# Local attention feeding a phase mixer on one core: q and k transposed by column halves, and the first attention and its loads reordered

## The chip, the core and the metric

The kernel runs on one core of one Trainium2 chip. The metric is the device time of one execution in microseconds (us); lower is better. A core has five engines that run beside each other, each through its own list of instructions in order: TensorE for matmuls (PE in the profile; PEld is its loading of weights), VectorE (DVE), ScalarE (ACT), GpSimd (POOL) and SyncE (SP). They meet through semaphores. DMA queues move data between device memory, the on-chip memory SBUF and back; matmul results land in PSUM, from where DVE or ACT must copy them. A tile here is a block of SBUF or PSUM with 128 partitions.

## What is computed

There are 4 batches of 8 heads, 768 tokens and 64 values per head. A token sees the first 8 tokens and the 96 latest ones (itself among them), with a bias that falls with the distance by a slope of the head. The attention's output, 512 wide, goes through a phase layer, a mix over tokens and a channel layer:

```python
scores = scale * q @ k.T + bias            # kept where global or local
a = softmax(scores); x = heads_to_columns(a @ v)
theta = x @ w_theta
zr, zi = x * cos(theta), x * sin(theta)
y = w_tok_r @ zr + w_tok_i @ zi            # over the 768 tokens
u = x + y
out = u + relu(u @ w_ch)
```

## The kernel before

Tokens are cut into 6 tiles of 128 and heads into 4 pairs; p is the pair. For a pair, q and k are brought into the form "two heads' 64 values on 128 partitions, tokens along the row" (qT and kT). Scores are made for 128 keys at a time against their own 128 queries and the next 128, with kG holding the keys of a tile with the 8 global keys copied over its first columns (`kglob`). One score block c covers two key tiles of both heads; ACT takes its exponential (`score_exp`, L302). `values` multiplies by v, which carries a column of ones, so that column 64 is the softmax's sum; DVE takes the reciprocal (L360) and multiplies (L362) into x. `xtrans` transposes x, `theta` multiplies by w_theta and takes cosine and sine on ACT (L395) and the products zri on DVE (L398), `mix` multiplies by the token weights (L409), and `utrans` and `chan` do the channel layer.

Batch 0's attention has an order written out by hand for all engines (the statements from `load_w()` to `manual.close()`). There the bias goes into PSUM as a matmul with a diagonal matrix (`diagonals`, `score_bias`, L275), ahead of the score matmuls (L295), which use the two halves of the array's rows, one head each. For pair 0, q and k come as fp32 through SP's and ACT's queues and are cast by DVE and ACT (`cast0`, L198); for pairs 1 to 3, they come as bf16 through POOL's queue, and `cast0` is a copy on DVE that puts the two heads beside each other per token tile. Then `turn0` (L204) transposes 128 x 128 blocks into PSUM, 6 for q and 6 for k, and `out0` (L211) copies them out, kT on ACT and qT on DVE. The bias tables for the later batches (`bias_table`, L142, eight activations) stand at the end, after the sines of batch 0.

Batch 1 to 3 are woven into the mixing of the batch before by `weave`, which deals side steps out by weights in proportion to the main steps; from `manual.close()` on a scheduler sets each engine's order within that, and `behind` keeps a preparation after the latest mix on its engine. Batches 1 and 2 prepare q and k with `prep`: `prep_copy` (L229, two DVE copies per pair, a pair ahead), 12 transposes (L244), the copies out (L249 on DVE, L251 on ACT) and `kglob` (L218, L220). Both batches' preparations fall into the mixing of batch 0. Batch 3 uses DMA transposes (`prep_dma`). Transposed blocks, mix sums and batch 0's values share four small PSUM buffers; score blocks use two large ones.

All large loads go through POOL's queue in program order: q, k, v of batch 0 by pieces, w_theta, the token weights (`load_w`, L159: three loads of two token tiles for each of the two matrices), w_ch (L162), then q and k of batch 1, v of batch 1, q and k of batch 2. A load waits for the one eight places before it. `trans_w` (L168, L169) transposes the token weights; tile 0 before theta, the others between mixes.

Of the kernel before, what the change touches and what calls it, by code (L numbers as in the profile page):

```python
# [9 lines left out]
FP = mybir.dt.float32  # L10
BF = mybir.dt.bfloat16
AF = mybir.ActivationFunctionType
# [4 lines left out]
def kernel(  # L17
# [13 lines left out]
    nc = tc.nc  # L31
    B, H, S, D = q.shape
    T = 128
# [103 lines left out]

    etab = const.tile([T, H, 5, T], BF)

    def bias_table(p):  # L140
        for h in (2 * p, 2 * p + 1):
            nc.scalar.activation(etab[:, h], dist[:, 0:5], AF.Exp, scale=-slopes[h])  # L142

    halfpi = const.tile([T, 1], FP)
    junk = const.tile([T, 1], FP)
# [8 lines left out]
    def load_w():  # L154
        nc.gpsimd.dma_start(out=w_theta_bf, in_=moe_w_theta.rearrange("(c p) n -> p c n", p=T))
        for tt in range(0, NT, 2):
            for wi, src in enumerate((moe_w_tok_r, moe_w_tok_i)):
                w2 = moe.tile([T, 2, S], BF, name="w_nat", bufs=6)
                nc.gpsimd.dma_start(  # L159
                    out=w2, in_=src[tt * T:(tt + 2) * T, :].rearrange("(a p) s -> p a s", p=T))  # L160
                w_nat[wi, tt], w_nat[wi, tt + 1] = w2[:, 0], w2[:, 1]
        nc.gpsimd.dma_start(out=w_ch_bf, in_=moe_w_ch.rearrange("(c p) n -> p c n", p=T))  # L162

    def trans_w(tt, copy=nc.vector.tensor_copy):
# [22 lines left out]
    def behind(eng):  # L187

        return tc.issue_after(anchor[eng]) if eng in anchor else nullcontext()

    tiles0 = {}

    def cast0(p, i_, eng, h=None):
        if (p, "n") not in tiles0:
            tiles0[p, "n"] = att.tile([T, NT, 2, 2, D], BF, name="qkn", bufs=2)
        src = qk32[:, i_] if p == 0 else loads[0][0][:, i_, 2 * p:2 * p + 2]
        hs = slice(0, 2) if h is None else slice(h, h + 1)
        eng(out=tiles0[p, "n"][:, :, i_, hs].rearrange("p t h d -> p h t d"), in_=src[:, hs])  # L198

    def turn0(p, i_):  # L200
        qkn = tiles0[p, "n"]
        ps = tiles0[p, i_] = ps_small([T, NT, T], BF)
        for t_ in range(NT):
            nc.tensor.transpose(ps[:, t_, :], qkn[:, t_, i_].rearrange("p h d -> p (h d)"), ident)  # L204

    def out0(p, i_, copy, half=None):
        to = qkT.setdefault((0, p), [None, None, None])
        if to[i_] is None:
            to[i_] = att.tile([T, S], BF, name=("qT", "kT")[i_], tag=("qT", "kT")[i_], bufs=6)
        ns = slice(0, T) if half is None else slice(half * T // 2, (half + 1) * T // 2)  # L210
        copy(out=to[i_].rearrange("p (n t) -> p n t", t=NT)[:, ns],  # L211
             in_=tiles0[p, i_].rearrange("p t n -> p n t")[:, ns])

    def kglob(b, p):
        kT = qkT[(b, p)][1]
        kG = qkT[(b, p)][2] = att.tile([T, NT - 2, T], BF, name="kG", bufs=6)
        with behind("dve") if b == B - 1 else nullcontext():
            nc.vector.tensor_copy(  # L218
                out=kG, in_=kT[:, T:(NT - 1) * T].rearrange("p (t n) -> p t n", t=NT - 2))
            nc.vector.tensor_copy(out=kG[:, :, 0:NG], in_=kT[:, None, 0:NG].to_broadcast([T, NT - 2, NG]))  # L220

    qkns = {}

    def prep_copy(b, p):
        qk = loads[b][0]
        qkn = qkns[b, p] = att.tile([T, NT, 2, 2, D], BF, name="qkn", bufs=2)
        with behind("dve"):
            for i_ in range(2):
                nc.vector.tensor_copy(  # L229
                    out=qkn[:, :, i_].rearrange("p t h d -> p h t d"), in_=qk[:, i_, 2 * p:2 * p + 2])  # L230

    def prep(b, p):
        if p == 0:
            prep_copy(b, 0)
        if p + 1 < NP:
            prep_copy(b, p + 1)
        qkn = qkns[b, p]
        qT = att.tile([T, S], BF, name="qT", bufs=6)
        kT = att.tile([T, S], BF, name="kT", bufs=6)
        for i_, dst in ((0, qT), (1, kT)):  # L240
            ps = ps_small([T, NT, T], BF)
            with behind("pe"):
                for t_ in range(NT):
                    nc.tensor.transpose(ps[:, t_, :], qkn[:, t_, i_].rearrange("p h d -> p (h d)"), ident)  # L244

            dst = dst.rearrange("p (n t) -> p n t", t=NT)
            src = ps.rearrange("p t n -> p n t")
            if i_ == 0:
                nc.vector.tensor_copy(out=dst, in_=src)  # L249
            else:  # L250
                nc.scalar.copy(out=dst, in_=src)  # L251

        qkT[(b, p)] = [qT, kT, None]
        kglob(b, p)
# [78 lines left out]
            nc.vector.tensor_copy(out=vG[:, hs], in_=vn[:, hs, 1:NT - 1, :])  # L333
        nc.vector.tensor_copy(out=vG[0:NG, hs], in_=vn[0:NG, hs, 0:1, :].to_broadcast([NG, n, NT - 2, D + 1]))

    def values(b, p, hh):
        vn = loads[b][1]
        e_t, vG = ebuf[(b, p)], vGs[b]
        h = 2 * p + hh
        if b == 0:  # L340
            po = ps_small([T, 1, 512], FP)
        else:
            if hh == 0:
                pos[(b, p)] = ps_big()
            po = pos[(b, p)][:, hh:hh + 1, :]
        for it in range(NT):
            mms = [(e_t[:, hh, it, 0, :], vn[:, h, it, :])]
            if it:
                mms.append((e_t[:, hh, it - 1, 1, :], vG[:, h, it - 2, :] if it > 1 else vn[:, h, 0, :]))
            o = po[:, 0, it * (D + 1):(it + 1) * (D + 1)]  # L350
            for i_, (l_, r_) in enumerate(mms):
                nc.tensor.matmul(o, lhsT=l_, rhs=r_, start=(i_ == 0), stop=(i_ == len(mms) - 1))  # L352
        if b and hh == 0:
            return
        if b:
            po = pos[(b, p)]
        h0, n = (hh, 1) if b == 0 else (0, 2)
        po4 = po[:, :, 0:NT * (D + 1)].rearrange("p a (t d) -> p a t d", d=D + 1)
        rec = att.tile([T, n, NT, 1], FP, name="rec", tag=f"rec{n}")
        nc.vector.reciprocal(rec, po4[:, :, :, D:D + 1])  # L360
        xv = x_sb[b][:, p, :, h0 * D:(h0 + n) * D].rearrange("p t (a d) -> p a t d", a=n)
        nc.vector.tensor_mul(xv, po4[:, :, :, 0:D], rec.to_broadcast([T, n, NT, D]))  # L362

    def xtrans(b, p, copy=nc.vector.tensor_copy):
        if b:
            anchor["sp"] = nc.sync.dma_start_transpose(
                out=xT_sb[b][:, p, :].rearrange("p (t s) -> p t s", t=NT),
                in_=x_sb[b][:, p].rearrange("p t d -> p (t d)")).ins
            return
        ps = ps_small([T, S], BF)  # L370
        for st in range(NT):
            nc.tensor.transpose(ps[:, st * T:(st + 1) * T], x_sb[b][:, p, st, :], ident)
        copy(out=xT_sb[b][:, p, :], in_=ps)


    zri, u_sb, uTs, pss, css = {}, {}, {}, {}, {}
# [68 lines left out]
    def load_all_qk(b):  # L445
        alloc_qk(b)
        load_qk(b, 0, 8)
# [54 lines left out]
            i_ += 1  # L502

    load_w()
    load_all_qk(1)
    load_all_v(1)
    load_all_qk(2)
    alloc_x(0)
# [1 line left out]
    warm(6)  # L510
    distances()
    diagonals(0)
    cast0(0, 1, dve, 0)
    cast0(0, 1, act, 1)
    turn0(0, 1)
    cast0(0, 0, dve, 0)
    cast0(0, 0, act, 1)
    turn0(0, 0)
    out0(0, 1, act, 0)
    out0(0, 1, dve, 1)  # L520
    out0(0, 0, act, 1)
    out0(0, 0, dve, 0)
    kglob(0, 0)
    score_bias(0, 0)
    score_bias(0, 1)
    score_mms(0, 0, 0)
    score_mms(0, 0, 1)
    score_exp(0, 0, 0)
    cast0(1, 1, dve)
    cast0(1, 0, dve)  # L530
    diagonals(1)
    turn0(1, 1)
    turn0(1, 0)
    for p in range(NP):
        nxt = p + 1 < NP
        score_exp(0, p, 1)
        if nxt:
            out0(p + 1, 1, act)
            out0(p + 1, 0, dve)
            kglob(0, p + 1)  # L540
        if p:
            values(0, p - 1, 0)
            values(0, p - 1, 1)
        score_bias(p, 2)
        score_mms(0, p, 2)
        score_exp(0, p, 2)
        if p + 2 < NP:
            cast0(p + 2, 1, dve)
            cast0(p + 2, 0, dve)
            diagonals(p + 2)  # L550
        if p == 0:
            vglob(0, 0, 4)
        if p == 1:
            vglob(0, 4, 4)
        if nxt:
            score_bias(p + 1, 0)
            score_mms(0, p + 1, 0)
            score_exp(0, p + 1, 0)
            score_bias(p + 1, 1)
            score_mms(0, p + 1, 1)  # L560
            if p + 2 < NP:
                turn0(p + 2, 1)
                turn0(p + 2, 0)
        if p:
            xtrans(0, p - 1, act if p == NP - 1 else dve)
    values(0, NP - 1, 0)
    values(0, NP - 1, 1)
    trans_w(0, nc.scalar.copy)
    xtrans(0, NP - 1)
    for c in range(NT // 2):  # L570
        theta(0, c, 0)
        theta(0, c, 1)
    for p in range(NP):
        bias_table(p)
    manual.close()
    for eng in (mybir.EngineType.PE, mybir.EngineType.DVE, mybir.EngineType.Activation):
        last = [i for i in nc.cur_bb.bb.instructions if i.engine == eng][-1]
# [82 lines left out]
```

The softmax here doesn't subtract the row's maximum and nothing guards it: scores larger than these inputs give would overflow.

## Time and profile before

| | us |
|---|---|
| median of 13 runs (lowest, highest) | 174.99 (174.42, 176.38) |
| profiled execution, its own time | 174.42 |
| its span | 172.4 |
| PE busy | 159.5 (93%) |
| DVE busy | 128.1 (74%) |
| ACT busy | 99.2 (58%) |
| first exponential starts (L302) | 9.37 |
| first theta matmul (L389) | 27.98 |
| first mix matmul (L409) | 33.16 |
| k of batch 1 landed (issued at 22.28) | 41.7 |
| first transposes of batch 1 (L244) | 41.67 |

Times of events are counted from the span's start. In a row of the timeline the numbers are the start and the time from the first start to the last end of a run of like instructions, then engine, line, operation, what is written and what is read, shapes and count; the bracket at the end is idle time before it and what ended it. A row of the groups ends in busy time, the mean of one in ns, and idle time with what ended it. Rows of tenths cut the span into 40 slices, each digit the busy share of one. A matmul's busy time is longer than its slot, since matmuls overlap in the array: slots are read from the distances between starts. The chain of waits follows the work that ended last back to the start.

### The profile page before, as it was taken

Reading aid. Unit: us, or ns where it says so; the run is one execution under the profiler, and the core shown is the slowest. Engines: PE = TensorE matmul, PEld = TensorE weight load, DVE = VectorE, ACT = ScalarE, POOL = GpSimd, SP = SyncE. Lnnn points to the kernel's source line nnn. Section 1 sums busy time; section 2 is a strip of 40 time slices with the busy share of each in tenths; the row PEclk is TensorE's granted clock in tenths of the full one; section 3 lists DMA queues with packets and bytes.
Section 4 is the critical chain, followed back from the end, with each engine's and each line's share of the span. In section 5 each row is a group of like instructions: output and inputs, shape, how many; then the busy total and the mean of one; then the engine's idle time right before and its main releaser. Section 6 shows DMA issues by size and latency. Waiting matters only on the chain.

```text
span 172.4 us, 3627 instructions
## 1 busy us (share of the span) xinstructions
PE 159.5 (93%) x1457; PEld 84.7 (49%) x1482; DVE 128.1 (74%) x288; ACT 99.2 (58%) x124; POOL 37.3 (22%) x45
## 2 busy tenths in 40 slices
PE   6789978999999999999999998999999989999991
PEld 1355655455756566544455463444554634444440
DVE  7578965677999999999587588597786837724443
ACT  2479676999497595489834740989348308500010
POOL 8983346005271110099100000000000000000000
PEclk9999999999999999999999999999999999999999
DMA  5999999999999999899999697787138571313335
GB/s 152 189 194 178 210 208 208 205 204 171 161 204 174 166 156 155 108 110 154 213 134 136 157 161 167 137 152 224 30 76 112 136 171 40 143 40 101 102 93 183
DMA packets 75088, 25.92 MB, mean 150 GB/s; under 512 B 63168, under 2 KB 72128, under 8 KB 75072
## 3 DMA queue, kind: packets, MB, share of 16 engines
q0 software_dynamic: 45680, 12.45, 78.2%
q1 hardware_dynamic: 28976, 12.72, 34.7%
q10 hardware_dynamic: 416, 0.52, 0.9%
q8 instruction: 11, 0.18, 0.4%
q14 instruction: 5, 0.04, 0.1%
HBM read 25.69 MB, written 6.29 MB: 185 GB/s over the span
## 4 chain that ended last, share of the span: by engine, by line
PE 49%; DMA 22%; DVE 19%; POOL 5%; issue 2%; ACT 1%; SPq 0%; DVEq 0%; POOLq 0%
PE ps L409 27%; DMA qk<-in_k_dram 11%; PE ps L434 9%; DMA w_nat<-in_moe_w_tok_r_dram 7%; PE pb L295 4%; PE pb L352 3%; PE pb L389 3%; DVE qT L249 3%; POOL qk L73 3%; DVE e L312 2%; DVE qkn L229 2%; PE ps L389 2%; DVE o_sb L440 2%; POOL vn L88 2%; DMA kT<-qk 2%
## 5 line engine op out<-in xcount | busy, mean ns | idle before, releaser
L409 PE MATMUL ps<-zri,w_tokT 128*128 128x512 bf16 x271 | 67.4, 379 | 1.5 <-issue 0.5
L302 ACT ACTIVATE e<-pb 128x1024 bf16<-128x1024 f32 (+1 forms) x48 | 43.6, 958 | 22.5 <-PE pb L295 22.3
L409 PEld LDWEIGHTS <-w_tokT 128*128 128x128 bf16 x288 | 26.1, 98 | 28.9 <-issue 1.0
L414 DVE TENSOR_TENSOR u<-x_sb,ps 128x512 bf16<-128x512 bf16 x24 | 16.4, 681 | 14.6 <-PE ps L409 12.7
L434 PE MATMUL ps<-w_ch_bf,uT 128*128 128x512 bf16 x94 | 23.9, 379 | 0.3 <-DVE u L414 0.2
L398 DVE TENSOR_TENSOR zri<-x_sb,cs 128x512 bf16<-128x512 bf16 x48 | 17.9, 416 | 7.8 <-ACT cs L395 7.6
L440 DVE SCALAR_TENSOR_TENSOR o_sb<-ps,u 128x512 f32<-128x512 f32 (+1 forms) x25 | 16.4, 661 | 3.1 <-PE ps L434 3.1
L395 ACT ACTIVATE cs<-pb,halfpi 128x1024 bf16<-128x1024 f32 x8 | 8.9, 1115 | 15.7 <-PE pb L389 15.7
L312 DVE TENSOR_TENSOR e<-e,etab 128x1024 bf16<-128x1024 bf16 (+1 forms) x24 | 14.7, 615 | 3.4 <-ACT e L302 3.4
L295 PE MATMUL pb<-qT,kT 64*128 64x128 bf16 x224 | 15.9, 223 | 0.8 <-ACT kT L211 0.3
L389 PE MATMUL pb<-w_theta_bf,xT 128*128 128x512 bf16 x62 | 15.0, 379 | 1.1 <-DMA xT<-x_sb 1.0
L295 PEld LDWEIGHTS <-kT 64*128 64x128 bf16 x224 | 9.0, 95 | 14.2 <-issue 13.0
L389 PEld LDWEIGHTS <-xT 128*128 128x128 bf16 x96 | 9.1, 98 | 11.9 <-DMA xT<-x_sb 2.2
L428 ACT COPY uT<-ps 128x512 bf16<-128x512 bf16 x7 | 4.1, 587 | 18.6 <-PE ps L427 18.6
L352 PEld LDWEIGHTS <-e 128*128 128x128 bf16 x352 | 12.7, 97 | 3.0 <-issue 1.0
L434 PEld LDWEIGHTS <-uT 128*128 128x128 bf16 x96 | 8.9, 98 | 10.0 <-ACT uT L428 0.3
L295 PE MATMUL pb<-qT,kG 64*128 64x128 bf16 x128 | 11.9, 220 | 0.3 <-DVE kG L220 0.3
L88 POOL DMA_DIRECT2D vn<-in_v_dram x5 | 9.6, 1928 | 11.8 <-DVE vn L68 10.2
L362 DVE TENSOR_TENSOR x_sb<-pb,rec 128x768 bf16<-128x768 f32 x12 | 11.4, 948 | 0.3
L315 DVE TENSOR_TENSOR e<-e,etab 128x1024 bf16<-128x1024 bf16 x12 | 8.2, 684 | 2.8 <-ACT e L302 2.8
L352 PE MATMUL pb<-vn,e 128*128 128x65 bf16 x168 | 9.6, 193 | 0.2
L251 ACT COPY kT<-ps 128x768 bf16<-128x768 bf16 x8 | 6.4, 798 | 5.1 <-PE ps L244 5.1
(74 smaller groups left out, 205.5 us busy)
## 6 DMA issues: line engine op xcount, KB each, us to landing
out_dram<-o_sb SPq DMA_DIRECT2D x23, 256.0 KB, 2.4
vn<-in_v_dram POOLq DMA_DIRECT2D x3, 768.0 KB, 22.8
qk<-in_q_dram POOLq DMA_DIRECT2D x2, 768.0 KB, 20.7
qk<-in_k_dram POOLq DMA_DIRECT2D x2, 768.0 KB, 23.4
w_nat<-in_moe_w_tok_r_dram POOLq DMA_DIRECT2D x3, 384.0 KB, 14.2
w_nat<-in_moe_w_tok_i_dram POOLq DMA_DIRECT2D x3, 384.0 KB, 15.4
vn<-in_v_dram POOLq DMA_DIRECT2D x2, 384.0 KB, 8.8
qk<-in_q_dram POOLq DMA_DIRECT2D x8, 96.0 KB, 9.3
```

What stands on the lines that cost most here:

```text
L88: nc.gpsimd.dma_start(out=vn[:, h0:h0 + n, :, 0:D].rearrange("p h t d -> p (h t) d"), in_=v[b, h0:h0 + n].rearrange("h (t p) d -> p (h t) ...
L295: nc.tensor.matmul(pb[:, hh, o:o + T], lhsT=lhsT, rhs=qT[R, (own, nxt)[part]], start=bool(b), stop=bool(b) or (jt == NT - 1 or (j == 1 and ...
L302: ins = nc.scalar.activation(e_c, pb[:, :, 0:n], AF.Exp, scale=scale).ins
L312: nc.vector.tensor_mul(e_c, e_c, tab[:, :, s0:s0 + n // T].rearrange("p a s n -> p a (s n)"))
L352: nc.tensor.matmul(o, lhsT=l_, rhs=r_, start=(i_ == 0), stop=(i_ == len(mms) - 1))
L362: nc.vector.tensor_mul(xv, po4[:, :, :, 0:D], rec.to_broadcast([T, n, NT, D]))
L389: nc.tensor.matmul(pb[j_] if last else pb[:, j_, :], lhsT=xT[:, dc, st(j_)], rhs=w_theta_bf[:, dc, :], start=(dc == 0), stop=(dc == NC - 1))
L398: nc.vector.tensor_mul(zri[b][:, i_, 2 * c + j_, :].rearrange("p (g d) -> p g d", g=NP), xb[:, :, 2 * c + j_, :], cs[:, i_, j_].rearrange( ...
L409: anchor["pe"] = nc.tensor.matmul(ps, lhsT=w_tokT[wi][:, st, tt * T:(tt + 1) * T], rhs=zri[b][:, wi, st, :], start=(st == 0 and wi == 0), ...
L414: anchor["dve"] = nc.vector.tensor_add(u_sb[b, tt].rearrange("p (g d) -> p g d", g=NP), x_sb[b][:, :, tt, :], ps.rearrange("p (g d) -> p g ...
L434: nc.tensor.matmul(ps_c, lhsT=uT[:, dc, :], rhs=w_ch_bf[:, dc, :], start=(dc == 0), stop=(dc == NC - 1))
L440: nc.vector.scalar_tensor_tensor(o_sb[:, cols], in0=ps_c[:, cols], scalar=0.0, in1=u[:, cols], op0=ALU.max, op1=ALU.add)
```

## The change

The copies that set two heads side by side (`prep_copy`, and `cast0` for pairs 1 to 3) are gone. A new function `turn` transposes each head's 64 columns by themselves, from the loaded tile into one half of PSUM's partitions, so there are 12 transposes of 128 x 64 in place of 6 of 128 x 128. Pair 0's cast goes to a tile of its own in the loaded layout. The bias matmuls of pair 0 move ahead of its transposes, pair 1's transposes ahead of the second score block, and the first two bias tables into the start of batch 0; `kglob` can be done for a part of the tiles. The last pair of batch 0 runs after the loop: values, x and its transpose are done for token tiles 0 to 3 and then for 4 and 5, with the first theta block around the second piece. The load of batch 1's q and k moves ahead of the last two token-weight loads and w_ch.

```diff
-    def bias_table(p):
-        for h in (2 * p, 2 * p + 1):
-            nc.scalar.activation(etab[:, h], dist[:, 0:5], AF.Exp, scale=-slopes[h])
+    def bias_table(h):
+        nc.scalar.activation(etab[:, h], dist[:, 0:5], AF.Exp, scale=-slopes[h])
...
                 w_nat[wi, tt], w_nat[wi, tt + 1] = w2[:, 0], w2[:, 1]
+            if tt == NT - 4:
+                load_all_qk(1)
...
+    def turn(ps, src):
+        for t_ in range(NT):
+            for hh in range(2):
+                nc.tensor.transpose(ps[hh * D:(hh + 1) * D, t_, :], src[:, hh, t_, :], ident)
 
     def turn0(p, i_):
-        qkn = tiles0[p, "n"]
         ps = tiles0[p, i_] = ps_small([T, NT, T], BF)
-        for t_ in range(NT):
-            nc.tensor.transpose(ps[:, t_, :], qkn[:, t_, i_].rearrange("p h d -> p (h d)"), ident)
+        turn(ps, loads[0][0][:, i_, 2 * p:2 * p + 2] if p else qk0[:, i_])
...
-    def prep_copy(b, p):
-        qk = loads[b][0]
-        qkn = qkns[b, p] = att.tile([T, NT, 2, 2, D], BF, name="qkn", bufs=2)
-        with behind("dve"):
-            for i_ in range(2):
-                nc.vector.tensor_copy(
-                    out=qkn[:, :, i_].rearrange("p t h d -> p h t d"), in_=qk[:, i_, 2 * p:2 * p + 2])
+    def prep(b, p):
+        qk = loads[b][0]
...
             with behind("pe"):
-                for t_ in range(NT):
-                    nc.tensor.transpose(ps[:, t_, :], qkn[:, t_, i_].rearrange("p h d -> p (h d)"), ident)
+                turn(ps, qk[:, i_, 2 * p:2 * p + 2])
...
-    load_all_qk(1)
     load_all_v(1)
...
     diagonals(0)
-    cast0(0, 1, dve, 0)
-    cast0(0, 1, act, 1)
+    score_bias(0, 0)
+    score_bias(0, 1)
+    cast0(1, dve, 0)
+    bias_table(0)
+    cast0(1, act, 1)
     turn0(0, 1)
...
-    kglob(0, 0)
-    score_bias(0, 0)
-    score_bias(0, 1)
+    kglob(0, 0, 0, 1)
     score_mms(0, 0, 0)
-    score_mms(0, 0, 1)
+    bias_table(1)
     score_exp(0, 0, 0)
-    cast0(1, 1, dve)
-    cast0(1, 0, dve)
-    diagonals(1)
+    kglob(0, 0, 1)
     turn0(1, 1)
     turn0(1, 0)
-    for p in range(NP):
+    score_mms(0, 0, 1)
+    diagonals(2)
+    diagonals(3)
+    for p in range(NP - 1):
...
+    p = NP - 1
+    score_exp(0, p, 1)
+    values(0, p - 1, 0)
+    values(0, p - 1, 1)
+    score_bias(p, 2)
+    score_mms(0, p, 2)
+    score_exp(0, p, 2)
+    values(0, p, 0, 0, 4)
+    values(0, p, 1, 0, 4)
+    xtrans(0, p - 1)
+    trans_w(0, act)
+    xtrans(0, p, dve, 0, 4)
+    theta(0, 0, 0)
+    values(0, p, 0, 4, 6)
+    values(0, p, 1, 4, 6)
+    theta(0, 0, 1)
+    xtrans(0, p, dve, 4, 6)
+    for c in range(1, NT // 2):
         theta(0, c, 0)
         theta(0, c, 1)
-    for p in range(NP):
-        bias_table(p)
+    for h in range(2, H):
+        bias_table(h)
```

## The prediction

> **What bounds the kernel now.** I read the rows of busy tenths first, then the windows by stage, then the timeline, the waits, and last the chain of waits.
>
> ```profile
> PE   6789978999999999999999998999999989999991
> DVE  7578965677999999999587588597786837724443
> ...
> PE 49%; DMA 22%; DVE 19%; POOL 5%; issue 2%; ACT 1%; SPq 0%; DVEq 0%; POOLq 0%
> ```
> ```profile
> 9.00:34.00 25.00, 22.41 (x290) 13.60 (x291) 18.69 (x52) 20.09 (x24) 11.17 (x13) 1.00 1.36 201
> 34.00:41.60 7.60, 7.45 (x53) 3.86 (x52) 5.84 (x14) 7.57 (x12) 2.21 (x1) 1.00 1.54 194
> 41.60:72.00 30.40, 29.05 (x371) 18.76 (x377) 30.30 (x70) 20.30 (x27) 6.56 (x8) 1.00 2.13 163
> 72.00:172.40 100.40, 94.43 (x723) 45.79 (x734) 67.25 (x135) 48.06 (x58) 9.15 (x10) 1.00 0.76 129
> ```
>
> The columns of the second view are stretch, length, then busy us of PE, PEld, DVE, ACT and POOL. TensorE (PE) is nearly full in every stretch. From 41.6 to 72.0 VectorE (DVE) is full too (30.3 of 30.4 us): both are at their limit. Half of the chain's 22% DMA is the load of batch 1's k (issued 22.28, landed 41.7), but PE had work until 41.67, so that share isn't idle PE time.
>
> A busy PE can hide waits, so I count starts in the timeline:
>
> ```profile
> 13.36 0.23 PE L295 MATMUL pb<-qT,kT 64*128 64x128 bf16 x2
> ...
> 13.42 0.22 PE L295 MATMUL pb<-qT,kG 64*128 64x128 bf16 x2
> ...
> 13.48 0.22 PE L295 MATMUL pb<-qT,kT 64*128 64x128 bf16 x2
> ...
> 13.54 0.22 PE L295 MATMUL pb<-qT,kG 64*128 64x128 bf16 x2
> 13.68 0.67 PEld L204 LDWEIGHTS <-qkn 128*128 128x128 bf16 x12
> 13.69 0.84 PE L204 MATMUL ps<-ident,qkn 128*128 128x128 bf16 x12
> ...
> 14.37 0.28 PE L352 MATMUL ps<-vn,e 128*128 128x65 bf16 x4
> ```
>
> The last four score pairs start 0.057 us apart: two matmuls on half the rows each run together. The 12 whole transposes take 14.37 - 13.69 = 0.68 us, 0.057 each. Between the last pair's slot (13.54 + 0.057) and the first transpose lie 0.09 us, and as much in the other direction: a change of array shape costs about 0.094. Matmuls over 512 columns start 0.216 apart, L352's 0.029.
>
> From the first mix (33.16) to batch 1's theta (72.09) the program has 85 matmuls over 512 columns (18.4 us), 96 transposes of q and k (5.4), 76 other transposes (4.2), 44 score pairs (2.5), 88 values matmuls (2.6) and 26 changes of shape (2.4): 35.6 of 38.9 us. So PE loses 3.3 us there. The same count leaves about 3.9 us lost from 10 to 30 us and about 3 from 75 on, which the change hardly touches. Extra PE work after 33 us is therefore paid almost in full.
>
> **The change part by part.** Everything is against this execution (174.42 us, span 172.4, 2.0 around it); the median of the 13 runs is 174.99, 0.57 above it.
>
> (1) Copies removed.
>
> ```profile
> L229 DVE COPY qkn<-qk 128x768 bf16<-128x768 bf16 x16 | 5.0, 339 | 0.1
> ```
> ```profile
> PEld L244 <- DVE qkn L229: 1.6, 3, 0.6
> ```
>
> 16 copies at about 0.3 us leave DVE in the full stretch, 5.0 us, and 6 more (2.5) leave the first attention. In the first, PE is the other limit: its starts slip by 1.0 us in all at the L244 groups that wait for L229 (0.14, 0.11, 0.11, 0.28, 0.39), and smaller slips follow the full DVE. I take 1.2 us gained. The bounds are 0 (new waits take their place: eight transposed tiles now stand close together, and each waits for one of four small PSUM buffers, whose emptying costs DVE 0.86 + 0.4 a pair against 0.7 of PE) and 2.3 (all but 1 us of the 3.3).
>
> (2) Column halves. Each tile's 6 transposes become 12 of 64 columns, two per token tile into the two halves of PSUM's partitions. No row shows that shape. Nearest from below is the score pair, two halves in 0.057: then 6 pairs cost what 6 whole transposes do, and nothing is added. From above, each half takes a whole slot: 0.112 a pair. I see no reason for a gain under the whole transpose's slot. After the first mix there are 16 x 6 = 96 pairs, so the bounds are 0 and 96 x 0.055 = 5.3 us. I take 0, since the score pair has the same number of instructions, the same 128 columns streamed and weights of the same size; the 5.3 stays in the range. The order of the built programs has 63 changes of shape after the first mix where before has 54: 9 x 0.094 = 0.85 us, unhidden (bounds 0 and 1.7, if a change to a column shape costs twice as much).
>
> The Trainium skill speaks against this part: "TensorEngine Tiling (Array Packing)", Restrictions, says that column tiling switches the fast weight load off. By "TensorE: Matmul & The Clock Gate", LDWEIGHTS, a plain load of 64 columns is an estimated 53 ns; two one after the other would make a pair 107 ns and this term +4.8 us, where the row gives 0. No run here shows it yet.
>
> (3) The first attention.
>
> ```profile
> 6.79 1.91 PE L275 MATMUL pb<-dist,diag 128*128 128x512 bf16 x4
> ...
> 21.69 1.94 ACT L302 ACTIVATE e<-pb 128x1024 bf16<-128x1024 f32 x2 [0.31 <-PE pb L295]
> ...
> 24.48 0.81 ACT L302 ACTIVATE e<-pb 128x768 bf16<-128x768 f32 x1 [0.86 <-PE pb L295]
> ...
> 25.21 0.51 PE L372 MATMUL ps<-ident,x_sb 128*128 128x128 bf16 x6 [0.77 <-DVE x_sb L362]
> ...
> 27.98 3.62 PE L389 MATMUL pb<-w_theta_bf,xT 128*128 128x512 bf16 x15
> ```
>
> Until about 10.2 us PE runs at half rate by its spacing (L275: 0.427 where it is 0.216 later), though the row of granted clock shows no dip. The four bias matmuls now fill 4.44 (diagonals ready) to 6.15, and the transposes start at 6.25 instead of 5.53. k and q are 12 pairs at 0.107, until 7.53; then come 0.3 of latency, ACT's half copy 0.48, DVE's 0.56, a one-tile kG at 0.2 and the scores: first exponential at 9.4, as now (9.37). Its bias table takes ACT's wait for the DMA (2.53 to 4.97) but for 0.1. Pair 1's 24 transposes now stand ahead of the second score block: up to 0.5 late while the clock is slow.
>
> From there the exponentials of pairs 0 to 3 now start at 9.37, 12.93, 16.7 and 21.69; ACT's own work is 2 x 0.97 + 0.84 + 0.80 = 3.6 a pair. The last step is 5.0 because DVE, in order, does 0.9 of casts and 0.28 of diagonals before pair 3's kG. Without them I place the four at 9.4, 13.2, 17.0 and 20.7, and the last exponential at 23.5 (now 24.48), since the second x transpose still stands ahead of it on PE.
>
> (4) The split. PE slips 0.84 at 24.2 (L372 waits for x_sb), 0.47 at 26.5 and 0.28 at 27.3. Now pair 3's tokens 0 to 511 need only the second exponential and fill the first gap. x of pair 2 is ready at 24.3, its copy at 26.0, and theta starts at 26.05 instead of 27.98, with 0.25 of values and a wait of about 0.25 for pair 3's x inside it. The last x copy stands on DVE behind four zri products that wait for ACT's first sines: theta ends at 31.9, not 33.1. The second mix step then waits some 0.3 for sines, which the later steps make up. Parts 3 and 4 together: 1.2 us gained. Bounds: 0.4 lost (the late second block is never caught up) and 2.4 gained (the clock rises a step earlier because the bias matmuls fill PE's idle 2 us, and all the slips go).
>
> (5) The load. The third token pair lands 3.7 us after the second (27.7 to 31.4) and w_ch 2.5 later. Moved ahead of those, k lands 6.2 earlier, at 35.5. PE reaches the first transpose 7.7 us after the first mix, at 39.6: nothing is gained over now, but unmoved it would cost 41.7 - 39.6 = 2.1. The token pair then lands at 39.2, needed after 50 (L168 at 53.97 now), and w_ch at 41.7, needed at 48 (L434 at 49.97 now); the issues behind them on POOL's queue keep their place. Cost 0. Six instead of eight bias tables after the sines relieve ACT by 1.3 us, which was late for nothing PE waits on: 0.
>
> Sum: -1.2 + 0 + 0.85 - 1.2 = -1.55, or 172.9 in this execution, and 173.4 beside the median.
>
> **The rivals.** *Halves don't overlap* (slower): at 0.112 a pair, PE pays 5.3 us between 39 and 72. The first attention has 48 pairs, 2.7 us more, of which its lost time hides about half, so part 3 ends at +0.3: 5.3 + 0.85 - 1.2 + 0.3 = +5.2, 180.2. For: PE has no slack there and no row shows the shape. Against: row halves overlap fully. It decides from 0.073 a pair (1.55 / 96 above 0.057); at 0.090 it gives about +1.9, 176.9. *The gain is bound elsewhere* (no change): the late second block and the sine chain leave part 3 and 4 at 0, and the crowded tiles leave 0.6 of part 1: +0.25, 175.2. For: ACT is at 20.1 of 25 us there. *All slips go*: -2.3 + 0.85 - 2.4 = -3.85, 171.1. For: PE's idle time before 5.5. Against: three engines are above 70% in 9 to 34. That the load does nothing by itself is part of the forecast.
>
> **How the numbers follow.** Forecast 0.52 (own range 172.4 to 174.5), all slips 0.08, bound elsewhere 0.14, halves not overlapping, wholly or partly, 0.26. The range 171.6 to 178.5 leaves out half of the third (0.04) and the upper part of the last (0.15). A measurement here can tell about 0.3%, 0.5 us. Faster: 0.47 of the forecast and 0.08, 0.55; same: 0.05 and 0.09, 0.14; slower: 0.26 and 0.05, 0.31.
>
> **What would show it.** The column transposes' pairs start 0.057 apart, twelve pairs in 0.7 us; 0.11 refutes part 2. The first mix starts at about 31.9, L229 is gone and the PE waits for DVE between 40 and 72 fall by 1 us; batch 1's theta starts 1 to 2 us earlier. A wait of the first prep for k, or of the late token tiles, would refute part 5; waits of PE for small PSUM buffers near 40 to 46 would show the crowding.

## The result and the profile after

The changed kernel takes 176.89 us (median of 11 runs, 175.66 to 178.03) against 174.99 before: a ratio of 1.0104, with a 95% interval of 1.0079 to 1.0128. It is 1% slower where 173.4 was forecast. Its profiled execution took 176.68 (span 174.7). All ratios here count only executions within 1.5% of the fastest of their kernel; longer ones, such as the profiled one of e11 below, are called slow and left out.

I cut the span at events that both programs have: the first mix, the first sine of batches 1, 2 and 3, and the last u. After the first mix TensorE has the same work in before and after except for the column halves, so the stretches can be compared. From batch 1's first sine on its order is the same too; ahead of it the scheduler gave it another one.

| us | first mix at | to sine of batch 1 | to batch 2 | to batch 3 | to the last u |
|---|---|---|---|---|---|
| before | 33.16 | 40.86 | 33.85 | 33.96 | 24.17 |
| after | 32.41 | 42.46 | 34.51 | 34.68 | 24.17 |
| difference | -0.75 | +1.60 | +0.66 | +0.72 | 0 |

The sum is +2.23, the spans differ by 2.25. So the first attention gained, and all three later stages lost, also the two in which the change alters no instruction of TensorE.

The row of busy tenths, the chain of waits and the stretches of the changed kernel (columns as before):

```profile
PE   6669899999998999799998998999999979999991
DVE  7564976866999999758577588597786827723443
...
PE 57%; DMA 18%; DVE 14%; ACT 4%; POOL 2%; issue 2%; SPq 0%; DVEq 0%; POOLq 0%; ACTq 0%
PE ps L399 27%; PE ps L424 9%; DMA xT<-x_sb 7%; DMA uT<-u 5%; PE pb L283 5%; PE pb L379 4%; DMA qk<-in_k_dram 4%; ACT cs L385 3%; PE pb L340 3%; PE ps L202 2%; PE ps L379 2%; PE pb L263 2%; DVE e L300 2%; DVE x_sb L351 2%; DVE zri L388 2%
```
```profile
9.00:34.00 25.00, 22.73 (x326) 13.52 (x331) 18.10 (x54) 20.27 (x25) 11.26 (x13) 1.00 1.38 200
34.00:41.60 7.60, 7.33 (x74) 4.31 (x75) 5.15 (x11) 6.80 (x11) 2.21 (x1) 1.00 1.45 196
41.60:72.00 30.40, 28.90 (x447) 18.12 (x452) 28.91 (x60) 20.34 (x26) 7.35 (x8) 1.00 2.07 165
72.00:174.70 102.70, 94.54 (x717) 45.30 (x730) 65.56 (x129) 46.68 (x56) 8.94 (x10) 0.99 0.78 125
```

The full stretch is DVE's limit no more (28.9 of 30.4), but PE hasn't become busier there. In the tenths, PE has a 7 in the 17th slice (70 to 74 us) where before had a 9. The chain now has DMA transposes of x and u in it; before, half of its DMA share was the load of k. The timeline of PE shows the place:

```profile
66.54 0.59 PE L399 MATMUL ps<-zri,w_tokT 128*128 128x512 bf16 x2
67.07 0.86 PE L202 MATMUL ps<-ident,qk 128*64 128x128 bf16 x24
67.86 1.04 PE L424 MATMUL ps<-w_ch_bf,uT 128*128 128x512 bf16 x3
68.83 0.86 PE L202 MATMUL ps<-ident,qk 128*64 128x128 bf16 x24
69.62 1.04 PE L399 MATMUL ps<-zri,w_tokT 128*128 128x512 bf16 x4
70.50 0.39 PE L417 MATMUL ps<-ident,u 128*128 128x128 bf16 x4
70.72 1.03 PE L399 MATMUL ps<-zri,w_tokT 128*128 128x512 bf16 x4
71.58 0.59 PE L379 MATMUL pb<-w_theta_bf,xT 128*128 128x512 bf16 x2
73.37 3.19 PE L379 MATMUL pb<-w_theta_bf,xT 128*128 128x512 bf16 x13 [1.19 <-DMA xT<-x_sb]
```

Two things are to be seen. The 24 column halves (12 pairs) take their slots in 67.86 - 67.07 less a change of shape, 0.058 a pair (neighbouring pairs start 0.056 apart): the halves overlap. And theta of batch 1 starts at 71.58, 0.5 earlier than before, does two matmuls, and then stands: 1.35 us lost by starts, until x of the third pair has landed. Before, x of that pair landed at 71.28, and PE came at 72.09. Now it landed at 73.32, although it was issued 2.3 us earlier (64.04, not 66.36).

The waits say how often. First the changed kernel, then the kernel before (us in all, times, longest):

```profile
PE pb L379 <- DMA xT<-x_sb: 2.7, 4, 1.2
...
PE ps L424 <- DMA uT<-u: 0.5, 1, 0.5
```
```profile
PE pb L389 <- DMA xT<-x_sb: 1.0, 2, 0.5
```

By starts the changed kernel loses to these waits 1.35 at 71.8, 0.67 at 93.8 (u), and 0.67 at 107.9, 141.0 and 142.5 each; before has 0.69 at 106.3 and 0.63 at 140.3 only. The new ones come to 1.35 + 0.67 + 0.72 = 2.74 of the 2.98 that the three stretches lost.

### The profile page after: what moved, and what is told of

It reads as the page before. It is cut to its first block, busy times and chain, and to the rows that moved or that the text cites. A ratio compares the mean times of both kernels' runs of the same rounds, so it can differ in the third digit from the quotient of the medians.

```text
span 174.7 us, 3894 instructions
## 1 busy us (share of the span) xinstructions
PE 159.3 (91%) x1600; PEld 83.4 (48%) x1626; DVE 123.5 (71%) x274; ACT 98.4 (56%) x123; POOL 38.0 (22%) x45
## 4 chain that ended last, share of the span: by engine, by line
PE 57%; DMA 18%; DVE 14%; ACT 4%; POOL 2%; issue 2%; SPq 0%; DVEq 0%; POOLq 0%; ACTq 0%
PE ps L399 27%; PE ps L424 9%; DMA xT<-x_sb 7%; DMA uT<-u 5%; PE pb L283 5%; PE pb L379 4%; DMA qk<-in_k_dram 4%; ACT cs L385 3%; PE pb L340 3%; PE ps L202 2%; PE ps L379 2%; PE pb L263 2%; DVE e L300 2%; DVE x_sb L351 2%; DVE zri L388 2%
## 5 line engine op out<-in xcount | busy, mean ns | idle before, releaser
L283 PE MATMUL pb<-qT,kT 64*128 64x128 bf16 x224 | 15.0, 219 | 2.7 <-DVE qT L213 1.3
L202 PE MATMUL ps<-ident,qk 128*64 128x128 bf16 x288 | 11.0, 221 | 1.4 <-DMA qk<-in_k_dram 1.1
L283 PE MATMUL pb<-qT,kG 64*128 64x128 bf16 x128 | 11.3, 216 | 0.2 <-DVE kG L224 0.2
L202 PEld LDWEIGHTS <-qk 128*64 128x64 bf16 x288 | 8.8, 109 | 5.4 <-issue 2.3
```

Source lines behind the costliest of these rows:

```text
L202: nc.tensor.transpose(ps[hh * D:(hh + 1) * D, t_, :], src[:, hh, t_, :], ident)
L283: nc.tensor.matmul(pb[:, hh, o:o + T], lhsT=lhsT, rhs=qT[R, (own, nxt)[part]], start=bool(b), stop=bool(b) or (jt == NT - 1 or (j == 1 and ...
```

## The experiments

Each ratio stands against the kernel before, run on the same chip. I began with theory D, **DMA engines**: POOL's loads keep them full until about 71 us, so that x's DMA transposes land near 73 whatever PE does. Its rivals: the **columns** themselves cost the time (C), the moved **load** does (L), or the **order** that the engines got (S). Theory F, **code fetch**, came after the first four runs.

### First set: one part at a time

e1_cols: the kernel before, with the prep of batches 1 and 2 as in the changed one (`prep_copy` and its calls go too).

```diff
...
-                for t_ in range(NT):
-                    nc.tensor.transpose(ps[:, t_, :], qkn[:, t_, i_].rearrange("p h d -> p (h d)"), ident)
+                turn(ps, qk[:, i_, 2 * p:2 * p + 2])
```

> The kernel before, with column-half transposes and no copies in the preps of batches 1 and 2 alone; its prologue, its token loop and its order of loads are those of before. Theory D (DMA engines): batch 1's theta cannot get going before the DMA transposes of x land, at about 73.3 us in both traces, because POOL's loads keep the DMA engines full until about 71; what DVE and PE save between 41 and 72 then turns into a wait there. It expects no change: 174.5 to 175.7. Theory C (columns cost more in this crowded stretch than 0.057 a pair and 0.09 a change of shape, and that is the whole loss): 176.5 to 177.2. The recorded forecast's own parts 1 and 2 (-1.2 and, for the fewer changes of shape, at most +0.85) would give 173.8 to 174.7.

Measured: 175.13, ratio 1.0012 (0.9986 to 1.0037).

e2_oldprep: the same edit the other way round, in the changed kernel (pair 0's tile then shares the buffers of the copies).

> The changed kernel with the preps of batches 1 and 2 as before (two DVE copies a pair, whole transposes); its first attention, split pair and order of loads stay. Theory D: the time when x of batch 1 has landed sets the stage, so this is within 0.6 of the changed kernel: 176.3 to 177.5. Theory C (columns are the loss): back to 175.0 or below, 173.5 if the new prologue keeps its 1.2 us.

Measured: 174.22, 0.9970 (0.9938 to 1.0001). Run again later (e16_oldprep_again) 174.57, 0.9965 (0.9940 to 0.9990; one of its twelve executions took 403.69, and no trace shows why).

> The kernel with the new prologue and the old preps once more, beside the run above: 174.0 to 174.6, the ratio to the kernel before 0.995 to 0.999 as in its two runs so far.

e3_load:

```diff
-            if tt == NT - 4:
-                load_all_qk(1)
...
     load_w()
+    load_all_qk(1)
     load_all_v(1)
```

> The changed kernel with q and k of batch 1 loaded where the kernel before loads them, behind the last token weights and w_ch. Recorded forecast, part 5: PE reaches the first prep at about 39.6 to 40.5 and k lands at 41.7, so the first prep waits 1 to 2 us. Theory D: that wait costs nothing at the end, since it is taken from the wait at batch 1's theta: 176.4 to 177.4. Theory L (the moved load is what harms, since it pushes the later loads and transposes): 174.5 to 175.5. Neither D nor L, waits paid in full: 178 to 179.

Measured: 176.97, 1.0122 (1.0073 to 1.0171). PE loses 1.08 at 41.0, for k, and takes it back from the wait for x.

e4_late3:

```diff
-            side.append((0, lambda: (alloc_qk(3), load_qk_tokens(3, 0, H // 2))))
+            side.append((0, lambda: alloc_qk(3)))
...
-            load_qk_tokens(b, H // 2, H // 2)
+            load_qk_tokens(b, 0, H)
```

> The changed kernel, in which the eight loads of the first half of batch 3's q and k (0.77 MB as written, from 46 to 71 us) are issued behind the gate with the second half. The instructions of PE, DVE, ACT and SP keep their order one for one. Theory D: the DMA engines are free of POOL's loads from about 64, the transposes of x of batch 1 land within 3 to 4 us of their issue, PE's wait of 1.2 at 72 goes, batch 1's first sine starts at about 73.4 instead of 74.9; then the loads behind the gate end some 8 us later (about 102 instead of 94.7) and the transposes of u in that stretch wait longer. If those waits are covered: 175.2 to 175.8; if they take all of it back: 176.9 or more, with the first sine early all the same. Theory S (the order that the engines got is the loss, not the DMA engines): the first sine stays at 74.9 and the time at 176.6 to 177.2.

Measured: 177.17 (174.46 to 179.95), 1.0050 (1.0006 to 1.0094). The ratio rests on four of twelve executions; the medians are 1.2% apart. The trace is of the shortest, 174.46. In it x of the third pair landed 2.8 us after its issue, the first sine came at 73.21, and theta ran through, as this row of the timeline shows:

```profile
71.28 3.62 PE L379 MATMUL pb<-w_theta_bf,xT 128*128 128x512 bf16 x15
```

D was right on the first stage: without the loads the wait goes. By the median the gain was given back, and the runs spread over 5 us; the loads behind the gate end later (97.0 for v, 94.7 in the changed kernel), but the one trace is of an execution that kept the gain, so what took it from the others isn't shown.

What the set says: L falls (e3 is as slow). The new prologue with the old preps is 0.3% faster than before, about 0.5 us (e2, e16). The columns alone cost nothing that shows (e1, +0.2 us), but 1.3%, about 2.3 us, on top of the new prologue (e2 against the changed kernel, by the ratios): neither C nor D explains that, since e1 has the same loads and the same order of PE after the first mix as e3, issued x's third transpose at 65.39 and had it at 71.12, where e3 issued it at 65.34 and had it at 73.56.

### Second set: code fetch

The trace's DMA records show what differs. The page's table of queues (packets, MB, share of 16 engines), before and then after:

```profile
q8 instruction: 11, 0.18, 0.4%
```
```profile
q8 instruction: 12, 0.20, 0.5%
```

These packets carry 16 KB of instructions; they come on average about every 250 of TensorE's matmuls and weight loads (135 to 356 in before and after), and each takes 0.9 to 1.9 us on its DMA engine. In the changed kernel one ran from 71.2 to 72.4; the sixteen parts of x's third transpose came in between 72.11 and 73.32, where they mostly come within 0.1 to 0.4. One at 139.8 to 140.7 goes with x's (139.97 to 141.82, the waits at 141 and 142.5). One at 90.6 to 92.1 stands ahead of u's (93.45 to 94.68, PE's wait at 93.8), but u lands there with the last part of POOL's load of v (94.69). In e5 below the last fetch is over at 87.65, and u is as late (94.19, v 94.22, 0.62 lost): that wait goes with D's loads, and isn't shown to be a fetch's. The column halves double the transposes' instructions (192 more in the preps, 96 in the prologue), so these packets come at other times. To test it I changed nothing but dummy instructions at the start, where PE waits anyway:

```diff
         for _ in range(n):
             nc.tensor.matmul(ps, lhsT=zero[:, 0:T], rhs=zero, start=True, stop=True)
+        for _ in range(16):
+            nc.tensor.matmul(ps[0:32, 0:48], lhsT=zero[:, 0:32], rhs=zero[:, 0:48], start=True, stop=True)
...
-    warm(6)
+    warm(4)
```

That is e5_pad28. e6_pad56 has 30 tiny matmuls of 32 columns, e7_pad84 three big ones and 45 such; e8_before12 is the kernel before with five big ones and seven of 48.

> The changed kernel, in which two of the six dummy matmuls at its start are replaced by sixteen tiny ones, so that 28 more instructions stand in TensorE's program ahead of the real work; every other instruction and its order are the same, and TensorE waits for the diagonals there anyway. Theory F (code fetch): TensorE's instructions come in packets of 16 KB, about one in 250 instructions, each 0.9 to 1.8 us on one DMA engine; in the changed kernel one starts at 71.2 and the DMA transpose of x that PE needs at 72 has its first part at 72.11 and its last at 73.32, one stands at 90.6 before u's transpose (lands 94.68) and one at 139.8 before x's (parts from 139.97 to 141.82). 28 instructions more move these three to about 69.4, 88.9 and 138.0: the first wait (1.2) goes, the one at 94 may go, the one at 141 may stay: 174.6 to 175.9. Theory D (POOL's loads keep the DMA engines full until 71, whatever TensorE's program is) and theory S (order): no change, 176.4 to 177.4.

Measured: 178.15, 1.0188 (1.0158 to 1.0218): a miss. 0.9 of it is in the first attention (first mix at 33.33), where the clock step came late. The fetch, moved back by that, ran from 70.6 to 71.8, and x landed at 72.72, but theta of batch 1 ran through: the 1.35 are gone. The rest of the miss lies behind batch 2's first sine, where two other fetches met batch 3's k and x (see the table below).

> As the run before, with 56 more instructions in TensorE's program instead of 28. Theory F: the three fetches come at about 69.0, 88.5 and 137.6: the waits at 72 and 94 go or shrink, the one at 141 may stay: 174.4 to 175.9. Theories D and S: 176.4 to 177.4.

Measured: 175.20, 1.0017 (0.9993 to 1.0041), a time as F expected. Its fetches from there on started at 69.4, 82.9, 93.2, 108.1, 123.5 and 136.3.

> As the runs before, with 84 more instructions in TensorE's program. Theory F: the three fetches come at about 67.7, 86.2 and 135.6, so that all three transposes are clear of them: 174.2 to 175.2, the fastest of the three. Theories D and S: 176.4 to 177.4.

Measured: 176.08, 1.0067 (1.0043 to 1.0090): less than the changed kernel, more than F expected; a fetch ran from 69.9 to 71.8, and theta waited 1.05.

> The kernel before, with 12 more tiny dummy instructions in TensorE's program at its start. Theory F: its fetches at 70.7 and 142.2 move to about 70.0 and 140.1, the second in front of the transpose of x that lands at 141.14 and that batch 3's theta waits for: slower by 0.5 to 1.2, 175.5 to 176.2. Theories D and S: no change, 174.7 to 175.4.

Measured: 174.97, 1.0026 (0.9999 to 1.0053): not shown. Its fetch started at 144.4, not at 140.1, in a profiled execution of 176.13, well above the median.

So dummy instructions alone take 0.9% off the changed kernel (1.0017 against 1.0104, about 1.5 us): D and S, which expected no change, fall as the whole cause. F's places were poor, since a fetch runs ahead of PE by an amount that I couldn't foresee.

### Third set: x by TensorE

e9_pe_xT is the changed kernel with this edit; e10_oldprep_pe_xT is e2's with the condition `p == 3`, e11_pe_xT_b1 the changed one with pairs 2 and 3 of batch 1 alone.

```diff
-        if b:
+        if b and not (p == 3 or (b, p) == (1, 2)):
             anchor["sp"] = nc.sync.dma_start_transpose(
...
-        copy(out=xT_sb[b][:, p, own], in_=ps[:, own])
+        (nc.scalar.copy if b else copy)(out=xT_sb[b][:, p, own], in_=ps[:, own])
```

> The changed kernel, in which x of the last pair of batches 1 to 3, and of the third pair of batch 1, is transposed by TensorE and copied by ACT instead of by a DMA (24 transposes of 128 columns more for TensorE, four DMA transposes fewer). Theory F+D (transposes by DMA land late at the ends of the stages, where POOL's loads or a code fetch stand in front of them): PE's waits for x of 1.35 at 72, 0.67 at 108 and 0.67 and 0.68 at 141 go, 24 x 0.057 = 1.4 us of PE work comes, and PE waits some 0.3 each time for ACT's copy: 174.2 to 175.4. Theory S (the order of the engines is the loss): at least the added work is paid, 177 to 178.5.

Measured: 176.44, 1.0101 (1.0066 to 1.0135): a miss. After 72 no wait for x is left, but 0.55 and 1.08 are lost at 114.0 and 115.4 for DVE's o_sb, 0.9 for x at 67, and 1.4 of work is added. The first mix came at 33.13: 0.5 of that stood at the first exponential already (9.74), ahead of the 3.4 us from 10.49 on in which the granted clock was 0.5.

> The run with the preps of batches 1 and 2 as before (174.22 in its run), in which x of the last pair of batches 1 to 3 is transposed by TensorE and copied by ACT. Theory F+D: its waits for x of 0.85 at 105 and 0.63 at 140 go, 18 x 0.057 = 1.0 us of PE work comes: 173.4 to 174.4. Theory S: 175 to 176.

Measured: 181.13, 1.0364 (1.0322 to 1.0407). Here the scheduler put batch 1's theta ahead of the last two preps and mixes; PE waited 3.4 for x at 71 and the first sine came at 80.61. It tells nothing about the theories.

> The changed kernel, in which only x of the third and last pair of batch 1 is transposed by TensorE and copied by ACT. Theory F+D: the wait of 1.35 at 72 goes and 0.7 us of PE work comes; what lands later in batches 2 and 3 falls as the code fetches fall, which this moves (24 more instructions of TensorE after 60 us): 175.4 to 176.6. Theory S: 177 to 178.

Measured: 176.65, 1.0114 (1.0076 to 1.0152), just above F's range. x by TensorE costs about what it saves.

### Fourth set: the fetch once more, and the first attention

e12_pad28b has the 28 instructions of e5 with five big dummies and 15 of 64 columns; e13_before56 and e14_oldprep56 have e6's 56 in the kernel before and in e2's.

> The changed kernel with 28 more dummy instructions of TensorE at its start as in the first of these runs, but made so that TensorE is busy until 4.0 us, so that the clock step should not come late (first exponential at 9.2 to 9.3, first mix near 32.4). Theory F (code fetch): the fetches move to about 69.4, 88.9 and 138.0, ahead of the transposes that they met: 174.6 to 176.3. If dummy matmuls themselves cost time, or the place of the fetches is nothing: 176.6 to 177.5.

Measured: 177.10, 1.0123 (1.0095 to 1.0151): a miss, and by its time alone the place of the fetches could be nothing. Its trace says otherwise: theta of batch 1 ran through (start 72.00, first sine 73.92), and a fetch came at 139.4 instead of 138.0 and met x: issued 137.41, landed 141.72, 0.45 and 0.99 lost at 141 and 142. Another ran from 110.03 to 111.00 and met batch 3's k (issued 107.70, landed 112.08, 2.8 us after issue in the kernel before). DVE stood for it ahead of o_sb, and PE lost 0.94 and 1.08:

```profile
112.11 0.29 DVE L224 COPY kG<-kT 128x512 bf16<-128x512 bf16 x1 [2.32 <-DMA kT<-qk]
```
```profile
113.80 1.02 PE L426 MATMUL ps<-w_ch_bf,uT 128*128 128x512 bf16 x4 [0.77 <-DVE o_sb L432]
115.74 1.02 PE L401 MATMUL ps<-zri,w_tokT 128*128 128x512 bf16 x3 [0.92 <-DVE o_sb L432]
```

> The kernel before with 56 more dummy instructions of TensorE at its start. Theory F: its fetches move to about 67, 95.4, 127 and 136.5, the last beside the transposes of x issued at 135.8 and 138.4, which it now misses: slower by 0.3 to 1.2, 175.2 to 176.2. If the place of the fetches is nothing: 174.5 to 175.2.

Measured: 175.80, 1.0049 (1.0028 to 1.0070), as F expected. A fetch ran from 138.0 to 138.9, and x, issued at 136.01, landed at 140.28, not after 2.7 us but 4.3. PE's timeline there:

```profile
138.84 0.81 PE L411 MATMUL ps<-zri,w_tokT 128*128 128x512 bf16 x3
139.49 0.59 PE L391 MATMUL pb<-w_theta_bf,xT 128*128 128x512 bf16 x2
140.32 1.04 PE L391 MATMUL pb<-w_theta_bf,xT 128*128 128x512 bf16 x4 [0.24 <-DMA xT<-x_sb]
142.23 0.61 PE L391 MATMUL pb<-w_theta_bf,xT 128*128 128x512 bf16 x2 [0.87 <-DMA xT<-x_sb]
```

The wait of the third row ends when its transpose lands, the fourth waits for the next one, which SP had to issue later behind it (139.43, 138.40 in the kernel before).

> The kernel with the new prologue and the old preps (174.22 in its run) with 56 more dummy instructions of TensorE at its start. In its trace no transpose of x lands late by a fetch, so theory F sees nothing to gain and a chance to lose: 174.2 to 175.6. If the place of the fetches is nothing: 173.9 to 174.6.

Measured: 174.61, 0.9974 (0.9956 to 0.9992): it doesn't tell the two apart.

e15_turn2_late is e2's kernel, with pair 2's transposes back behind pair 1's scores:

```diff
-        if p + 2 < NP:
+        if p and p + 2 < NP:
             turn0(p + 2, 1)
...
         score_mms(0, p + 1, 1)
+        if not p:
+            turn0(2, 1)
+            turn0(2, 0)
```

> The kernel with the new prologue and the old preps, in which TensorE transposes pair 2's q and k behind pair 1's first two score blocks, as the kernel before did, instead of ahead of them. If TensorE's wait for pair 2's k (landed at 12.14) is what held the first attention: pair 1's first exponential at about 12.9 to 13.2 instead of 13.96, the first mix at 31.7 to 32.2 instead of 32.55, and 173.4 to 174.2 if the end keeps it. If ACT or DVE holds the first attention anyway: the first mix stays at 32.4 to 32.7 and the time at 174.0 to 174.8.

Measured: 174.11, 0.9952 (0.9929 to 0.9975): faster than both kernels, but by the time alone not told apart from e16, the same kernel without this edit, run beside it. The exponentials of pairs 1 and 2, first in the changed kernel, then in e15:

```profile
13.96 1.94 ACT L290 ACTIVATE e<-pb 128x1024 bf16<-128x1024 f32 x2 [1.20 <-PE pb L283]
16.46 0.84 ACT L290 ACTIVATE e<-pb 128x768 bf16<-128x768 f32 x1
18.07 1.94 ACT L290 ACTIVATE e<-pb 128x1024 bf16<-128x1024 f32 x2 [0.77 <-PE pb L283]
```
```profile
13.15 1.94 ACT L305 ACTIVATE e<-pb 128x1024 bf16<-128x1024 f32 x2 [0.39 <-PE pb L298]
16.18 0.81 ACT L305 ACTIVATE e<-pb 128x768 bf16<-128x768 f32 x1 [0.40 <-PE pb L298]
17.84 1.94 ACT L305 ACTIVATE e<-pb 128x1024 bf16<-128x1024 f32 x2 [0.85 <-PE pb L298]
```

Pair 1 starts 0.8 earlier, pair 2 0.2, the first mix comes at 32.18 (32.55 in e2, 32.44 in e16).

### All traces together

Of 405 DMA transposes issued between 94 and 150 us in 17 of the traces (e11's left out), 76 landed late (over 3.4 us for x, q and k, where 2.7 is usual; over 3.1 for u, usual 2.4). From issue to landing, one of TensorE's code packets ran beside 72 of the 76, and beside 36 of the 329 in time. Of x's alone, the 33 with a packet landed after 2.73 to 4.58 us, 22 of them after more than 3.4; the 79 without one all landed within 3.04. At 72, x's third landed 0.92 to 0.94 us after a fetch's end in the changed kernel, e3, e5, e6 and e12 (ends from 70.54 to 72.64); in the kernel before it landed at 71.28, while one ran (70.66 to 71.64). That ties nearly every late transpose to a fetch; that it is the cause rests on e5 to e7, e12 and e13, whose only edit is dummy instructions.

Whether a late one costs anything depends on what waits for it: x's third and last ones have no slack, and behind a late k of batch 3, PE lost 1.9 in e5 and 2.0 in e12 for o_sb, where it loses 0.4 in the kernel before. The next table takes each stretch of these runs and subtracts PE's waits over 0.3 us for x, u and o_sb behind 66 us, by starts:

| us | to sine of batch 1 | to batch 2 | to batch 3 |
|---|---|---|---|
| before | 40.86 | 33.85 - 0.69 = 33.16 | 33.96 - 1.04 = 32.92 |
| after | 42.46 - 1.35 = 41.11 | 34.51 - 1.34 = 33.17 | 34.68 - 1.75 = 32.93 |
| e5_pad28 | 41.11 | 34.44 - 1.28 = 33.16 | 36.28 - 3.37 = 32.91 |
| e6_pad56 | 41.11 | 33.86 - 0.71 = 33.15 | 35.36 - 2.45 = 32.91 |
| e7_pad84 | 42.16 - 1.05 = 41.11 | 34.53 - 1.36 = 33.17 | 33.90 - 0.98 = 32.92 |
| e12_pad28b | 41.09 | 33.96 - 0.81 = 33.15 | 36.39 - 3.46 = 32.93 |
| e13_before56 | 40.62 | 34.37 - 1.21 = 33.16 | 34.77 - 1.84 = 32.93 |

Behind batch 1's first sine, the kernels and the runs with dummies differ by these waits and by nothing else over 0.02 us.

## Why the prediction was wrong, step by step

**(1) Copies removed: -1.2 forecast, about -0.4 to -0.7 by a count of starts.** The built programs have equal work from the first mix to batch 1's first sine but for 35 changes of shape instead of 26, +0.85, and the order that the scheduler gave them. Where theta didn't wait for x, columns against old preps gave: e1 against before, 41.56 - 40.86 = +0.70; e4, e6 and e12 (40.93, 41.11, 41.09) against e2 and e14 (40.31, 40.37), +0.56 to +0.80. The starts part this: the nine changes are paid at 0.094 each, the column groups take 0.34 more than 0.056 a pair, mostly because the first pair behind a change takes 0.08, and what is left of the stretch, without slots (33.71), changes and waits for x, falls from 4.16 to 4.26 (e2, e14 to e16) to 3.59 to 3.78 (after, e4 to e7, e12). The pair of e1 and before alone would tell little: with the order of before, e13 took 40.62 and e8 41.57. So the copies, with the order that came with their going, gave 0.4 to 0.7 of the 1.2, and the rest of the waits for L229 was replaced. These are e1's, in that stretch:

```profile
PE pb L284 <- DVE x_sb L351: 0.4, 1, 0.4
PE ps L225 <- DVE qT L238: 0.3, 1, 0.3
...
PE pb L284 <- ACT e L291: 0.2, 1, 0.2
PE ps L225 <- DVE w_tokT L169: 0.2, 1, 0.2
```

VectorE was full, and its relief moved the waits more than it took them away.

**(2) Column halves: 0 forecast, +0.34 counted; the +0.85 was paid.** A pair takes 0.056, and the rival that halves don't overlap is refuted, though slower, its direction, is what came. Together, (1) and (2) were put at -0.35 and came to +0.56 to +0.80.

The 107 ns a pair estimated from the Trainium skill ("TensorEngine Tiling (Array Packing)", Restrictions, with "TensorE: Matmul & The Clock Gate", LDWEIGHTS) is not what this trace shows, with two weight loads of 128 x 64 in each 56 ns. What fell is "one after the other": two loads of the estimated 53 ns beside each other would fit 56 as well, so the trace doesn't tell whether the fast load was off.

**(3)+(4) First attention and split: -1.2 forecast, -0.75 measured, and not from where it was forecast.** The first exponential was placed right (9.4; 9.21). The last was to start 1.0 earlier (23.5) and came 0.2 later (24.66; 24.48 before): part (3) gained nothing. From there to the first mix, 8.4 was forecast and 7.75 measured (8.68 before): the split gave 0.9. That the sum is near is luck. Pair 1's exponential was placed at 13.2 and came at 13.96: the step left out that pair 2's transposes now stand ahead of pair 1's scores and wait for POOL's load of k, which landed at 12.14. The row of the waits:

```profile
PE ps L202 <- DMA qk<-in_k_dram: 1.1, 1, 1.1
```

e15 takes that away, and pair 1 starts at 13.15, as placed; 0.3 to 0.4 of the first mix comes back (against e16 and e2).

**(5) The load: 0, right.** k landed at 35.20 (35.5 forecast), PE came at 40.49. Unmoved, it costs 1.1 in its place (2.1 forecast) and nothing at the end (e3).

**The sum's scope.** The step that failed most is a half sentence: "about 3 from 75 on, which the change hardly touches". The sum ended at batch 1's theta as if everything behind it kept its distance, and it had no term for when x lands, at theta or behind it. x's transposes are DMAs, with 2.7 us from issue to landing at best and up to 9.5 while POOL's loads run (58.40 to 67.94 in the changed kernel); at batch 1's theta the issue came earlier, but the landing later. With the code fetches where the added instructions put them, x was late at 72 and at 141, +1.35 and +0.72; u, late with POOL's load of v, added +0.67 at 93.8. That is more than everything that was won. No rival had this; "bound elsewhere" came nearest, but looked for it in ACT's sines.

Without those three the changed kernel would stand at about 176.68 - 2.74 = 173.9 in its profiled execution, 0.5 below the one before. That is worked out, not run: e6, which still loses 1.04 at 140.7, is at 175.20, no different from before. It also lost 1.41 at 112 and 114 for o_sb, behind u and k that met the fetch at 108.1. What stays open is where a fetch will fall (F's times were hit in two of six runs, e6 and e13), and how the 1.35 at 72 divide between the fetch and the loads, since e4 ended the wait by the loads and e5, e6 and e12 by dummies.

## What to carry to other kernels

A gain ahead of a wait for a DMA is only a gain if the DMA starts earlier and lands earlier: look at its issue and its landing, not at the engine that waits. Dummy instructions alone moved the changed kernel by almost 1% either way (1.0017 and 1.0188, where it stands at 1.0104), so before a part that adds instructions is blamed, run it again with a few dummies where the engine waits. And an engine that is full isn't yet the one that others wait for: the waits on the removed line bound the gain from above, and here others took their place.

## What the runs showed of the hardware

A matmul with a 128 x 64 weight tile into one half of PSUM's partitions runs beside its neighbour into the other half: pairs 0.056 us apart, weight loads included, as fast as whole 128 x 128 transposes. A change to or from this shape costs about 0.09 like the one to row halves, and the first pair behind it takes 0.08.

TensorE's code comes in 16 KB packets over one DMA engine, 0.9 to 1.9 us each; of the 33 transposes of x between 94 and 150 us that met one, 22 landed after 3.4 to 4.6 us, where those that met none took 2.7 to 3.04.

The step of TensorE's clock from half to full spacing came by 6.3 us in the changed kernel, but only past 11.1 in e5, where a second group of 24 column transposes, from 9.67 on, takes 1.49 us like the first. The first ones, in the changed kernel, then in e5 (0.86 and 1.49 us for the same 24):

```profile
6.25 0.86 PE L202 MATMUL ps<-ident,qk 128*64 128x128 bf16 x24
```
```profile
6.28 1.49 PE L204 MATMUL ps<-ident,qk 128*64 128x128 bf16 x24
```

The bias matmuls ahead of them start at 4.47 after a gap of 0.54, in e5 at 4.46 after 0.63; that this is the reason isn't shown. e2 and e16 are one program, with a gap of 0.53 in both, and the same 24 take 0.86 from 5.96 in the one and 1.04 from 6.28 in the other. In e2 the spacing falls to half once more from 9.16 to 12.1. That is another thing: there the profile shows a granted clock of 0.5 from 8.98 for 3.4 us, while e5's shows none below 1.0 ahead of the end.
